# A state-space and token-mixing block: the second quarter of the input by GpSimd, the third quarter and one block of modulation weights at other places

## Chip, cores, metric

The kernel runs on one core of one Trainium2 chip. The metric is device microseconds from the launch to the end. Five engines work side by side: TensorE (PE: matmuls, with its weight loads as PEld), VectorE (DVE), ScalarE (ACT), GpSimd (POOL) and SyncE (SP), which here only issues DMAs. GpSimd issues a few DMAs too. All DMAs run on the core's 16 DMA engines, and so do the packets that bring each engine its instructions.

## What is computed

The reference, cut to what matters here (L = 2048 tokens, D = 448 channels, N = 256 states, F = 1792):

```python
mod = (silu(c) @ w_mod).reshape(1, 6, 1, 448)           # sa, ca, ga, sb, cb, gb
h = layernorm(x) * (1 + ca) + sa
K = 2 * real(einsum("dn,dnl->dl", C, exp(A * dt * pos)))   # one kernel of length L per channel
y = irfft(rfft(h) * rfft(K)) + h * D_skip                # per channel, over the tokens
x = x + ga * y
h = layernorm(x) * (1 + cb) + sb
x = x + gb * (w2.T @ gelu(w1.T @ h + b1) + b2)           # over the tokens
```

## The kernel before

The first half makes the 448 convolution kernels K. Channels are taken 16 at a time in 28 groups, each in two halves of the states: 56 steps, in sets of 8 (`BATCH`). A set begins with a *window* (`window`, slots e = 0 to 7): TensorE makes exponents (`st_exponents`, L621), ScalarE takes Exp of them into `mag` (L644), GpSimd makes `m2` from `mag` (`st_mag2`, L660 and L665), and VectorE does statistics and parameter work between. Then come the set's eight *steps* (`st_step`). In each, ScalarE turns two PSUM tiles of phases, `xe` and `xg`, into sines and cosines (L677 to L682). GpSimd makes the tile `G` (L684, L685), and VectorE makes the tile `E` (L686, L687, then whatever `between` holds, then L689, L690). TensorE makes the next step's phases (`st_phase`, L621) and, two steps later in the first set, 64 small products of E and G (`st_kgen`, L711).

The order on TensorE, VectorE, ScalarE and GpSimd is the order in which the code is written. In this part SP's is too. An engine that waits holds up everything behind it, and a DMA of SP or GpSimd is issued only when its turn comes in that engine's row.

The input x (2048 x 448) is loaded into one tile `xt`, as 16 rows of 128 x 448, in four quarters of four rows: `x_load(r0, n, eng)` issues four DMAs (one for each 32 partitions) of n rows each. Before the change the quarters go out like this. Rows 0 to 3: by GpSimd in `first_chain`. Rows 4 and 5, then 6 and 7: by SP in two calls, ahead of the first window. Rows 8 to 11 and 12 to 15: by GpSimd, behind steps 1 and 2 of the first set (steps count from 0). The layer norm's statistics of a row (`u_stats`, L513 and L514 on VectorE) are placed by hand: rows 0 to 3 in slots 4 to 7 of the first window, rows 2s and 2s + 1 inside step s for s = 2 to 7, by `between`, in the middle of VectorE's work on that step.

The modulation weights come in six blocks of 448 x 448 (`wm_load`). Block 1 is loaded by SP ahead of the first window; block 2 from the table `late`, which runs an entry at the head of step s, here s = 4; block 0 at s = 7. `modulation(k, half)` uses block 1 at steps 4 and 5, block 2 at steps 6 and 7 (L502 and L498 on TensorE). The tables `lph` and `lex`, which TensorE reads for phases and exponents, come by small SP DMAs in between (L607, L611), some of which wait until TensorE has left the buffer.

The second half of the program (inverse transform, second layer norm, the two matmuls with w1 and w2) is untouched by the change.

Of the kernel before, what the change touches and what calls it, by code (L numbers as in the profile page):

```python
# [220 lines left out]
def tile_adaln_s4d_mixer(ctx, tc, i, out):  # L221
# [20 lines left out]
    with ExitStack() as es:  # L242
        V, S, G, T = nc.vector, nc.scalar, nc.gpsimd, nc.tensor
# [53 lines left out]
        def x_load(r0, n, eng=nc.sync):  # L297
            for g in range(4):
                to = xt[32 * g : 32 * g + 32, r0 : r0 + n, 0:D]
                eng.dma_start(to, x.rearrange("(n g r) d -> g n r d", g=4, r=16)[g, :, r0 : r0 + n])  # L300
# [22 lines left out]
        def wm_load(k, tile):  # L323
            wms[k] = tile
            nc.sync.dma_start(wms[k], i["w_mod"][:, k * D : (k + 1) * D].rearrange("(q p) d -> p q d", p=PP))
# [11 lines left out]
        def wm_slot(k):  # L337
            w = wm0.rearrange("p k d -> p (k d)")[0:PP]
            return w[:, 4 * D * (k % 4) : 4 * D * (k % 4 + 1)].rearrange("p (q d) -> p q d", q=4)
# [1 line left out]


        late = {
            4: lambda: wm_load(2, wm_slot(2)),
            7: lambda: wm_load(0, wm_slot(0)),
            6: lambda: [
                nc.sync.dma_start(wu, i["WU"]),
# [114 lines left out]
        def logs(root=False):  # L462

            for a, s, u, xa, ya in tmp.values():
                S.activation(u, ya, AF.Square)
                S.activation(s, s, AF.Ln)
                S.activation(u, u, AF.Ln, bias=1.0)
            if root:
                S.activation(rs, mv[:, :, 1], AF.Ln, bias=eps_t)
                S.activation(rs, rs, AF.Exp, scale=-0.5)  # L470
            for q, (a, s, u, xa, ya) in tmp.items():
                S.activation(a, a, AF.Exp, bias=ldt[:, q : q + 1])
            tmp.clear()

        def angle():

            for a, s, u, xa, ya in tmp.values():
                S.activation(xa, ya, AF.Arctan)
# [134 lines left out]
        def load(g, exps):  # L613
            load_up(g, exps)
            load_lo(g, exps)
# [323 lines left out]
        par_load(1, par_names[2:4])  # L939
        for g in (1, 2):  # L940
            load(g, False)
        x_load(4, 2)
        x_load(6, 2)
        wm_load(1, wm_slot(1))
        remainder()

# [13 lines left out]
        def more(n):  # L960

            for _ in range(n):
                if next(rest, None) in ("logs", "end"):
                    return
# [26 lines left out]
        def window(s):  # L991
            if s:
                aside.append(True)
            angle()
            logs(s == 8)
            if s == 8:
                u_scale()
                u_table(0)
                u_table(1)

            if s == 0:
                st_exponents(s)
            for e in range(BATCH):
                st_exp(s + e)

                if e + 1 < BATCH:
                    st_exponents(s + e + 1)
                else:
                    st_phase(s)
                mellow()  # L1010
                flush(dve)
                flush(act)
                if s == 8 and e == 0:
                    tt(mod[1], mod[1], mod[2], ALU.mult)
                if s < 32:
                    more(WPACE[s // 8][e])
                if s == 0 and e >= 4:
                    u_stats(e - 4)
                if s == 8 and e in (3, 4):
                    modulation(0, e - 3)  # L1020
                if s == 8 and e == 5:

                    G.tensor_tensor(mod[0], mod[0], mod[2], ALU.mult)
                if s and e < (2 if s <= 32 else 1):
                    st_kgen(s - (2 if s <= 32 else 1) + e)
                elif e == 5:
                    if s == 8:
                        yks[0] = y0.tile([P, 32, DC], F32, tag="yk", name="yk0")
                    st_s1(s > 16)

                for k, e0 in ((4, 1), (5, 3), (3, 6)) if s == 16 else ():
                    if e in (e0, e0 + 1):
                        modulation(k, e - e0)

                if s == 8:
                    warm(7)
                if s in (8, 16):
                    some(u_rows, rows, (2, 2, 2, 2, 2, 0, 1, 1)[e])
                elif s == 24 and e != 5:
                    some(u_cols, cols, 1)  # L1040

                if s >= 40 and e == 2:
                    piece(False, True)
                if s >= 40 and e == 4:
                    piece(pieces[0] < NP, True)
                if s == 0 and e > 1:
                    st_mag2(e - 2)
                elif s and (e < 2 or s >= 32):
                    st_mag2(s + e)
                if s == 0 and e == 3:  # L1050
                    for r in range(4):
                        dsk_copy(r)
            aside.clear()
            if s == 0:

                S.activation(one, one, AF.Sin)
# [6 lines left out]
        for s in range(tail):  # L1063
            if s == 32:
                early.close()
                fp = es.enter_context(tc.tile_pool(name="fp", bufs=2))
                m2p.append(right("m2l", BATCH - 3))
                yks[1] = fp.tile([P, 32, DC], F32, name="yk1", bufs=1)
                for n in range(3):
                    pc_load(n)  # L1070
            if s % 2 == 0 and 0 < s and s // 2 + 2 < NG:
                load(s // 2 + 2, False)
            if s == 8:
                first.close()
            if s in late:
                late[s]()
            if s < NHALF and s % BATCH == 0:
                window(s)
                if s == 0:
                    gp_ = right("gp", 3)  # L1080
            if s % BATCH == 4:
                for g in range(s // 2 + 2, min(s // 2 + 6, NG)):
                    load(g, True)

            def between():
                flush(dve)
                if 2 <= s < BATCH:
                    for r in range(2 * s, 2 * s + 2):
                        u_stats(r)
                if s < len(pace):  # L1090
                    more(pace[s])

            mellow()
            if s >= NHALF:
                flush(dve)
                mellow()
            else:
                if s < 32 and s % BATCH > 1:
                    st_kgen(s - 2)
                if s % BATCH < 2:  # L1100
                    warm(10)
                if (s + 1) % BATCH:
                    st_phase(s + 1)
                elif s + 1 < NHALF:
                    st_exponents(s + 1)
                if s == 7:
                    warm(10)

                if s > 32 and s % BATCH:
                    st_kgen(s - 1)  # L1110
                st_step(s, between)
            flush(act)
            if s == NHALF:
                st_kgen(s - 1)


            if s in (1, 2):
                x_load(4 + 4 * s, 4, G)
            free = s > 7 and not st_s1(s % BATCH == BATCH - 1)
            if s + 2 < 32 and (s + 2) % BATCH > 1 and s + 2 > 5:  # L1120
                st_mag2(s + 2)

            if 3 < s < 8:
                modulation(s // 2 - 1, s % 2)
            if s == 7:
                par_load(2)

            if 8 <= s < 16 and free:
                some(u_rows, rows, 2 if s % 2 else 3)
            if s == 12:  # L1130
                par_load(3)
            if s == 16:
                spec.close()
                up = early.enter_context(tc.tile_pool(name="up", bufs=2))
                for n in range(4):
                    u_load(n)
            if 17 <= s < 32 and free:
                some(u_cols, cols, 2 if s < 24 else 3)
            if s == 31:
                flush(dve)  # L1140
                flush(act)
            if s > 32:
                piece(pieces[0] < NP and (s % 2 == 1 or s >= NHALF))
            if s == 34:

                for t in (ft, b1, b2):
                    V.memset(t, 0.0)
                nc.sync.dma_start(ft, i["FT"])
                nc.sync.dma_start(b1, i["B_b1"].rearrange("(t p) -> p t", p=P))
                nc.sync.dma_start(b2, i["B_b2"].rearrange("(t p) -> p t", p=P))  # L1150
# [52 lines left out]
    with ExitStack() as es:  # L1203
        es.enter_context(tc.manual_schedule(engines={ENG.PE, ENG.Activation, ENG.DVE, ENG.Pool}))
        V, S, G = nc.vector, nc.scalar, nc.gpsimd
# [192 lines left out]
```

## Time and profile before

| what | value |
|---|---|
| time, median of 3 runs | 698.07 us (697.39 to 699.43) |
| the profiled execution | 699.5 us, its span 697.7 us |
| busy: PE, PEld | 646.5 us (93%), 486.1 us (70%) |
| busy: DVE, ACT, POOL | 424.1 us (61%), 448.5 us (64%), 274.7 us (39%) |
| moved by DMA | 128.04 MB, mean 184 GB/s |
| granted TensorE clock, mean | 0.988 |

Rows in order of time give the start, the length, the engine, the line and operation, the tile written and those read, shapes, and in brackets how long the engine was idle before and what released it. A group's row gives totals instead. `L300` is line 300 of the kernel before. "issue" as a releaser means that the engine waited for nothing that the profile names. The rows of a table by stretches give, for each engine, busy time and instructions, then TensorE's granted clock, the busy share of the DMA engines and GB/s.

### The profile page before, as it was taken

How to read it: one execution, taken by the hardware profiler on the slowest of the kernel's cores; microseconds unless marked ns; L12 is line 12 of the kernel's file. 1: busy time of each engine (PE TensorE's matmuls, PEld its weight loads, DVE VectorE, ACT ScalarE, POOL GpSimd, SP SyncE). 2: the span in 40 equal slices, each digit the busy share in tenths (PEclk: the TensorE clock that was granted, in tenths of full speed). 3: DMA queues.
4: the chain of work that ended last, by engine and by line, in shares of the span. 5: the costliest groups of instructions: out<-in, count | busy, mean ns of one | idle time of the engine just before them, and what ended most of it. 6: DMA issues, size and time to landing. Idle time of an engine off the chain costs nothing.

```text
span 697.7 us, 18532 instructions
## 1 busy us (share of the span) xinstructions
PE 646.5 (93%) x7314; PEld 486.1 (70%) x7314; DVE 424.1 (61%) x811; ACT 448.5 (64%) x841; POOL 274.7 (39%) x364
## 2 busy tenths in 40 slices
PE   0868999999988899999999989999999999999997
PEld 0444454455545676676789747778999999999996
DVE  7877889787575584857744368777622354444431
ACT  5787698899879899999766568877422332222220
POOL 6694669588588767777546200000000000000000
PEclk9998999999999999999999999999999999999999
DMA  7595647588785486554579899974683445555640
GB/s 183 178 194 143 214 163 241 212 234 268 213 266 165 126 170 170 145 157 120 142 235 301 257 278 244 236 177 135 174 247 108 146 132 159 159 158 165 169 129 28
DMA packets 101894, 128.04 MB, mean 184 GB/s; under 512 B 13547, under 2 KB 85231, under 8 KB 101807
## 3 DMA queue, kind: packets, MB, share of 16 engines
q1 hardware_dynamic: 100606, 123.31, 63.0%
q0 software_dynamic: 1200, 3.54, 2.4%
q8 instruction: 58, 0.95, 0.6%
q14 instruction: 30, 0.24, 0.1%
HBM read 91.46 MB, written 34.87 MB: 181 GB/s over the span
## 4 chain that ended last, share of the span: by engine, by line
PE 68%; ACT 10%; DMA 8%; DVE 6%; issue 4%; POOL 3%; SPq 1%; DVEq 0%; ACTq 0%; POOLq 0%
PE xe L621 7%; PE acc L1222 7%; PE o L1365 6%; PE o L1364 6%; PE o L1366 6%; PE acc L1223 6%; PE acc L1224 6%; PE kg L711 6%; DMA si<-in_SK_dram 3%; PE xg L621 3%; PE pu L542 2%; PE pu L574 2%; PE vv L820 2%; PE kx L804 2%; PE vv L821 2%
## 5 line engine op out<-in xcount | busy, mean ns | idle before, releaser
L206 ACT CAST whi<-w 128x896 fp32r<-128x896 f32 x64 | 59.8, 938 | 134.9 <-PE o L1365 84.6
L215 DVE TENSOR_TENSOR wlo<-w,whi 128x896 fp32r<-128x896 f32 x64 | 68.1, 1088 | 43.1 <-ACT whi L206 36.8
L684 POOL TENSOR_TENSOR G<-mag,gs 128x512 f32<-128x512 f32 x56 | 71.9, 1283 | 50.9 <-ACT gs L680 47.1
L1222 PE MATMUL acc<-h3h,whi 128*128 128x448 f32 x224 | 82.7, 369 | 0.8 <-ACT h3h L1273 0.8
L1223 PE MATMUL acc<-h3l,whi 128*128 128x448 f32 x224 | 81.5, 364 | 0.7 <-DVE h3l L1280 0.5
L1365 PE MATMUL o<-ul,whi 128*128 128x448 f32 x224 | 81.3, 363 | 0.0
L1364 PE MATMUL o<-uh,whi 128*128 128x448 f32 x224 | 81.2, 362 | 0.0
L1224 PE MATMUL acc<-h3h,wlo 128*128 128x448 f32 x224 | 80.7, 360 | 0.0
L1366 PE MATMUL o<-uh,wlo 128*128 128x448 f32 x224 | 80.6, 360 | 0.0
L711 PEld LDWEIGHTS kg<-E,G 128*32 128x32 f32 x3584 | 56.6, 114 | 32.3 <-issue 22.2
L711 PE MATMUL kg<-E,G 128*32 128x64 f32 x3584 | 66.4, 228 | 6.7 <-issue 6.1
L685 POOL TENSOR_TENSOR G<-mag,gs 128x512 f32<-128x512 f32 x56 | 71.8, 1282 | 0.0
L621 PE MATMUL xg<-tab,lph 64*128 64x512 f32 x112 | 62.3, 556 | 5.1 <-ACT gs L680 2.4
L621 PE MATMUL xe<-tab,lph 64*128 64x512 f32 x112 | 62.2, 555 | 1.1 <-ACT gs L681 0.9
L686 DVE TENSOR_TENSOR E<-m,xe 128x512 f32<-128x512 f32 x53 | 36.4, 687 | 41.3 <-ACT xe L679 24.3
L1368 DVE SCALAR_TENSOR_TENSOR y<-o,b,mod 128x448 f32<-128x448 f32 x16 | 10.9, 684 | 80.2 <-PE o L1366 80.2
L665 POOL TENSOR_TENSOR m<-mag,w 128x512 f32<-128x512 f32 x53 | 56.0, 1056 | 4.3 <-DMA u<-us_d 0.2
L1222 PEld LDWEIGHTS acc<-h3h,whi 128*128 128x128 f32 x224 | 42.0, 188 | 13.9 <-ACT h L1278 5.6
L812 DVE TENSOR_TENSOR z<-kx,u 128x448 f32<-128x448 f32 x48 | 28.4, 620 | 27.7 <-PE kx L804 27.7
L1223 PEld LDWEIGHTS acc<-h3l,whi 128*128 128x128 f32 x224 | 42.1, 188 | 3.3 <-DVE h3l L1280 0.8
L1364 PEld LDWEIGHTS o<-uh,whi 128*128 128x128 f32 x224 | 42.0, 188 | 3.4
L621 PE MATMUL xe<-tab,lex 64*128 64x512 f32 x56 | 28.9, 531 | 16.6 <-DMA lex<-wm 15.8
(233 smaller groups left out, 1512.1 us busy)
## 6 DMA issues: line engine op xcount, KB each, us to landing
w<-in_B_w_dram SPq DMA_DIRECT2D x64, 224.0 KB
w<-in_B_w_dram SPq DMA_DIRECT2D x32, 448.0 KB
u<-us_d SPq DMA_DIRECT2D x48, 224.0 KB
yu_d<-yt SPq DMA_DIRECT2D x16, 448.0 KB
yi<-yu_d SPq DMA_DIRECT2D x32, 224.0 KB
us_d<-uo SPq DMA_DIRECT2D x16, 448.0 KB
v_d<-vt SPq DMA_DIRECT2D x32, 224.0 KB
vt<-v_d SPq DMA_DIRECT2D x16, 448.0 KB
```

The lines of the kernel that those rows point to most:

```text
L206: self.nc.scalar.copy(hi, w)
L215: eng.tensor_tensor(lo, w, hi.bitcast(F32), ALU.subtract)
L621: T.matmul(out[k], lhs[r], rhs[r], start=start, stop=stop)
L684: G.tensor_tensor(Gt[:, 1], mg_, v32(sg), ALU.mult)
L685: G.tensor_tensor(Gt[:, 0], mg_, v32(cg_), ALU.mult)
L711: T.matmul(kg[32 * q : 32 * q + 32, m], Gt[:, c, d], E[:, c, d], start=h == 0 and c == 0 and m == 0, stop=h == 1 and c == 1, skip_group_ch ...
L1222: nc.tensor.matmul(acc[f], hi[:, fs], h3h[:, r], start=r == 0, stop=False)
L1223: nc.tensor.matmul(acc[f], hi[:, fs], h3l[:, r], start=False, stop=False)
L1224: nc.tensor.matmul(acc[f], lo[:, fs], h3h[:, r], start=False, stop=r == 15)
L1364: nc.tensor.matmul(o, hi[:, ks], uh[kh][:, k], start=kh == 0 and k == 0, stop=False)
L1365: nc.tensor.matmul(o, hi[:, ks], ul[kh][:, k], start=False, stop=False)
L1366: nc.tensor.matmul(o, lo[:, ks], uh[kh][:, k], start=False, stop=kh == 1 and k == 6)
```

## The change

Three places of the code change, and a fourth is only written anew. SP no longer loads rows 4 to 7: GpSimd does, in slot 6 of the first window, four rows a DMA. Rows 8 to 11 are loaded behind step 0 instead of step 1. Rows 12 to 15 stay behind step 2 (8 + 2 x 2 = 12). Block 2 of the modulation weights is loaded at the head of step 3 instead of step 4.

```diff
         late = {
-            4: lambda: wm_load(2, wm_slot(2)),
+            3: lambda: wm_load(2, wm_slot(2)),
...
             load(g, False)
-        x_load(4, 2)
-        x_load(6, 2)
         wm_load(1, wm_slot(1))
...
                     more(WPACE[s // 8][e])
+                if s == 0 and e == 6:
+                    x_load(4, 4, G)
                 if s == 0 and e >= 4:
                     u_stats(e - 4)
...
-            if s in (1, 2):
-                x_load(4 + 4 * s, 4, G)
+            if s in (0, 2):
+                x_load(8 + 2 * s, 4, G)
```

In GpSimd's row, the end of the first window: each pair of L660 and L665 makes one step's `m2` (steps 3 and 4 here; steps 3 to 5 keep it in a part of the tile `wm`).

```order
 L660 TENSOR_TENSOR w<-mag 128x16
 L665 TENSOR_TENSOR wm_79<-mag,w 128x512
+L300 DMA xt<-in_A_u_dram 32x4x448 x4
 L660 TENSOR_TENSOR w<-mag 128x16
 L665 TENSOR_TENSOR wm_79<-mag,w 128x512
```

Four DMA issues now stand ahead of the pairs of steps 4 and 5.

GpSimd's row in the first steps, from step 0's G on (a pair of L684 and L685 is one step's G):

```order
 L684 TENSOR_TENSOR G<-mag,gs 128x512
 L685 TENSOR_TENSOR G<-mag,gs 128x512
-L684 TENSOR_TENSOR G<-mag,gs 128x512
-L685 TENSOR_TENSOR G<-mag,gs 128x512
 L300 DMA xt<-in_A_u_dram 32x4x448 x4
 L684 TENSOR_TENSOR G<-mag,gs 128x512
 L685 TENSOR_TENSOR G<-mag,gs 128x512
+L684 TENSOR_TENSOR G<-mag,gs 128x512
+L685 TENSOR_TENSOR G<-mag,gs 128x512
 L300 DMA xt<-in_A_u_dram 32x4x448 x4
 L684 TENSOR_TENSOR G<-mag,gs 128x512
```

The third quarter's four issues moved from behind step 1's G to behind step 0's; the fourth quarter's stay behind step 2's.

SP's row from the last table load ahead of the first window to the tables of the second set (`wm_79` from `in_w_mod` is a block of modulation weights, `lph` and `lex` are tables):

```order
 L611 DMA lph_144<-pars_57 64x1x256
-L300 DMA xt<-in_A_u_dram 32x2x448 x8
 L325 DMA wm_79<-in_w_mod_dram 112x4x448
 L607 DMA lph_142<-pars_57 32x256
 L611 DMA lph_142<-pars_57 64x1x256
+L325 DMA wm_79<-in_w_mod_dram 112x4x448
 L607 DMA lph_143<-pars_57 32x256
 L611 DMA lph_143<-pars_57 64x1x256
-L325 DMA wm_79<-in_w_mod_dram 112x4x448
 L607 DMA lex_145<-pars_57 32x256
```

The eight input issues are gone, and block 2 stands ahead of one pair of table loads that it stood behind.

## Prediction

> **What bounds the kernel now.** I read the page first (engines, DMA queues, chain), then the waits of the early stretch, then each engine's rows in order of time. The page's rows for the engines, the instruction queue and the chain:
>
> ```profile
> PE 646.5 (93%) x7314; PEld 486.1 (70%) x7314; DVE 424.1 (61%) x811; ACT 448.5 (64%) x841; POOL 274.7 (39%) x364
> ...
> q8 instruction: 58, 0.95, 0.6%
> ...
> PE 68%; ACT 10%; DMA 8%; DVE 6%; issue 4%; POOL 3%; SPq 1%; DVEq 0%; ACTq 0%; POOLq 0%
> ```
>
> PE carries two thirds of the chain, but the change touches only the first 65 us, where the input and the modulation weights come in. So that stretch has to be read by itself. The longest waits between 36 and 63 us (engine, line, what it waited for; total, times, longest):
>
> ```profile
> DVE st L513 <- DMA xt<-in_A_u_dram: 4.6, 1, 4.6
> PE kg L711 <- issue: 4.2, 1, 4.2
> ```
>
> VectorE waits once for input rows. The rows in order of time show where: L686 opens the VectorE part of a step, and L513 is the statistics of one input row.
>
> ```profile
> 37.92 0.69 DVE L686 TENSOR_TENSOR E<-m,xe 128x512 f32<-128x512 f32 x1 [0.41 <-ACT xe L679]
> ...
> 39.12 0.62 DVE L513 BATCH_NORM_STATS2 st<-xt 128x6 f32<-128x448 f32 x1
> ...
> 45.62 0.68 DVE L686 TENSOR_TENSOR E<-wm,xe 128x512 f32<-128x512 f32 x1
> 46.22 0.68 DVE L687 SCALAR_TENSOR_TENSOR E<-mag,xe 128x512 f32<-128x512 f32 x1
> 51.52 0.63 DVE L513 BATCH_NORM_STATS2 st<-xt 128x6 f32<-128x448 f32 x1 [4.62 <-DMA xt<-in_A_u_dram]
> ...
> 54.18 0.68 DVE L686 TENSOR_TENSOR E<-wm,xe 128x512 f32<-128x512 f32 x1
> ...
> 62.94 0.69 DVE L686 TENSOR_TENSOR E<-m,xe 128x512 f32<-128x512 f32 x1 [0.99 <-issue]
> ```
>
> The reader is to see the beat: steps 2 and 3 together take 45.62 - 37.92 = 7.70 us, 3.85 each, and VectorE never pauses in them. Step 4 takes 8.56, because at 46.90 the third quarter of the input (rows 8 to 11) is not there. The second quarter was needed at 39.12 and was there. VectorE sets the pace here, so these 4.62 us are on the path, unless something else is late at the same moment. Something is: the chain of waits shows TensorE stopped for nearly the same time.
>
> ```profile
> 48.06 0.88 PE kg L711 x58
> 48.93 4.23 issue
> 53.16 0.43 PE kg L711 x6
> ```
>
> It stops after 58 of 64 products of one step and waits for nothing that the profile names. The page has 58 instruction packets of 0.95 MB together, 16.4 KB each; 14,628 matmuls and weight loads over 58 are 252 instructions a packet. The DMA rows (packets, MB, share) of the stretches 37 to 40 and 40 to 50 us, and the instruction row of 50 to 52; queue 0 is GpSimd's, queue 1 SP's, queue 8 TensorE's instructions:
>
> ```profile
> q1 hardware_dynamic: 430, 0.74, 88.2%
> q8 instruction: 1, 0.02, 1.9%
> ```
> ```profile
> q0 software_dynamic: 281, 1.06, 56.5%
> q1 hardware_dynamic: 658, 0.97, 50.1%
> q14 instruction: 1, 0.01, 0.4%
> ```
> ```profile
> q8 instruction: 1, 0.02, 4.1%
> ```
>
> No instruction packet moves from 40 to 50, and the next comes just before TensorE resumes. In the stretches 37 to 44 and 44 to 49 it ran (matmuls, then loads):
>
> ```profile
> 37.00:44.00 7.00, 5.29 (x142) 3.50 (x135) 6.49 (x14) 6.78 (x15) 6.99 (x11) 0.92 1.01 236
> 44.00:49.00 5.00, 4.93 (x118) 3.09 (x110) 2.87 (x6) 3.73 (x9) 4.99 (x5) 0.77 1.08 204
> ```
>
> That is 505 instructions, two packets' worth, with one packet in. So I read the 4.23 us as instructions queued behind the same loads. Both stalls have one cause: too many bytes asked for at once.
>
> **The change part by part.** GpSimd's rows in time order, from the end of the first set to the fourth quarter's issue:
>
> ```profile
> 26.80 0.42 POOL L660 TENSOR_TENSOR w<-mag 128x16 f32<-128x16 f32 x1
> ...
> 28.63 1.05 POOL L665 TENSOR_TENSOR wm<-mag,w 128x512 f32<-128x512 f32 x1
> 31.09 1.27 POOL L684 TENSOR_TENSOR G<-mag,gs 128x512 f32<-128x512 f32 x1 [1.42 <-ACT gs L680]
> 32.32 1.32 POOL L685 TENSOR_TENSOR G<-mag,gs 128x512 f32<-128x512 f32 x1
> 35.13 1.29 POOL L684 TENSOR_TENSOR G<-mag,gs 128x512 f32<-128x512 f32 x1 [1.48 <-ACT gs L680]
> 36.37 1.29 POOL L685 TENSOR_TENSOR G<-mag,gs 128x512 f32<-128x512 f32 x1
> 37.60 2.20 POOL L300 DMA_DIRECT2D xt<-in_A_u_dram  x4
> 39.81 1.29 POOL L684 TENSOR_TENSOR G<-mag,gs 128x512 f32<-128x512 f32 x1
> ...
> 42.26 2.20 POOL L300 DMA_DIRECT2D xt<-in_A_u_dram  x4
> ```
>
> *GpSimd's queue.* Four issues cost 2.20 us of it. The second quarter now goes out at 26.8; the two m2 pairs behind it end at 29.68 + 2.20 = 31.9, and step 0's G starts 0.8 late and ends near 34.4. The third quarter follows, 34.4 to 36.6 (before, 37.6 to 39.8). Step 1's G ends near 39.1 (before, 37.66), step 2's starts there (before, 39.81), and the fourth quarter goes out at 41.6 (before, 42.26). So TensorE gets step 1's G about 1.4 us later, behind VectorE's beat, which turns to the next step only near 41.8 (37.92 + 3.85) anyway; from step 2 GpSimd is 0.7 us ahead. I cost this at nothing; without that cover it is 1.4 us.
>
> *SP's queue,* from the same view:
>
> ```profile
> 29.45 0.54 SPq L611 DMA_DIRECT2D lph<-pars  x1
> 30.03 6.09 SPq L300 DMA_DIRECT2D xt<-in_A_u_dram  x8
> 36.16 0.43 SPq L325 DMA_DIRECT2D wm<-in_w_mod_dram  x1
> ...
> 39.55 0.46 SPq L325 DMA_DIRECT2D wm<-in_w_mod_dram  x1
> ```
>
> Eight issues of 6.09 us go. The first weights (modulation 1) leave at 30.0, not 36.2. Modulation 2's leave after the two lph loads of step 2, which wait for TensorE to leave that buffer (about 33), so near 34, not 39.55: now ahead of the third quarter.
>
> *The bytes.* Slices of 5 us; the last three columns are TensorE's granted clock, the DMA engines' busy share and GB/s:
>
> ```profile
> 30.00:35.00 5.00, 4.49 (x24) 2.19 (x22) 4.36 (x6) 4.06 (x10) 2.55 (x2) 1.00 0.67 176
> 35.00:40.00 5.00, 4.78 (x144) 3.36 (x144) 4.55 (x10) 4.78 (x11) 4.86 (x7) 1.00 0.62 172
> 40.00:45.00 5.00, 3.29 (x72) 2.28 (x71) 4.90 (x11) 4.37 (x9) 4.99 (x7) 0.79 1.08 218
> 45.00:50.00 5.00, 3.93 (x81) 2.21 (x75) 1.90 (x4) 4.17 (x9) 4.92 (x6) 0.87 1.06 190
> ```
>
> The engines are two thirds busy from 30 to 40 and full from 40 to 50, at 204 GB/s on average. The change adds no byte; it fills the slack. In the new order, from about 29 us: a quarter of the input (128 x 4 x 448 x 4 B = 0.92 MB), two weight blocks (112 x 4 x 448 x 4 B = 0.80 MB each), the third quarter (0.92 MB): 3.44 MB, with some 0.15 MB of lph loads. At 204 GB/s that is 17.6 us, so the third quarter lands near 46.6, against 46.9 when VectorE asks. Bounds from the nearest rows: at 218 it is 45.5, at 190 it is 47.9. So the wait of 4.62 becomes 0 to 1.0; I take 0.3, and the term is **-4.3 us**. The second quarter goes out 26.8 to 29.0 with at most the first weights beside it, 1.72 MB, which 204 GB/s moves by 37.4; it is needed at 39.12. I cost that at nothing; at 172 GB/s it is 39.0, still in time.
>
> *TensorE's instructions.* This is the term that comes back. The packet that came at 37 to 40 was asked for when the engines had about one weight block ahead; now it meets what is left of 3.44 MB. By 36.7 some 7.7 us x 204 = 1.57 MB are through, so 1.9 MB stand ahead of it. Before, the second packet was asked for, by my reading, one packet's worth of instructions (252) ahead of the stop at 48.9, near 43.5 (44 to 49 holds 228). It met modulation 2's weights and the third and fourth quarters, 2.64 MB, less 3.5 us x 218 = 0.76 that were through: 1.9 MB too. It moved after 50, some 6.5 us later. If the first is as late, it moves near 43.2, and TensorE, which resumed up to 3.2 us after the slice's start at 50, has it by 43 to 46.4, where 43.4 is when it needs it: 0 to 3.0 us lost, of which about 1 is cover (the next tiles are ready for VectorE that long before its turn). The second packet, asked for at 43.5 to 45, meets about 1.4 MB (rest of the third quarter, the fourth, table loads): 1.4/1.9 x 6.5 = 4.8 us, so TensorE goes on near 51.5, where VectorE's beat without a stall has room until about 49.5 (45.62 + 3.85). The two overlap, so the later one counts: 0 to 4 us, and I take **+1.9**, half of the stop that the trace shows.
>
> *Half clock.* The granted clock was 0.79 and 0.87 in those slices and 1.00 around them. A shorter stop may spare some of it; step 7's 0.99 us wait (L686 at 62.94) came behind that. Bounds 0 to -1.0; I take **-0.2**.
>
> *Weights of modulation 2* are used by TensorE only at step 6, behind step 4's stall; moving the load costs nothing by itself beyond the bytes above.
>
> **Sum:** -4.3 + 1.9 - 0.2 = -2.6 us. The profiled execution took 699.5 us (span 697.7), so 696.9; the median of the three runs is 1.4 below it, 698.07, so 695.5. The rest of the chain follows in order behind this stretch, so I let the gain pass to the end.
>
> **The rivals.**
>
> *A, instructions never wait.* The trace shows 10 us without an instruction packet under full DMA engines. [...] As a mechanism of this kernel: if the stop at 48.9 was an accident of one engine's backlog, only VectorE's wait counted and all of it goes: 4.62 plus up to 1.0, 692.5 to 693.5. For it: a packet did come within 37 to 40 at 88% busy.
>
> *B, the stall moves.* The third quarter lands no earlier in effect, or both instruction packets are as late as before: TensorE then resumes near 53 as now, and 4.3 comes back whole: 697 to 699. For it: the bytes are the same, and modulation 2's weights are now ahead of the third quarter.
>
> *C, slower.* The place is TensorE's first packet, in step 3. If it waits as the longest shown (10 us from the 37 to 40 slice, so until 47 to 48), TensorE stops for 4 to 5 us at 43.4, the second packet is asked for only then and meets the fourth quarter: another 5 us, until 56 to 57 instead of 53.16: 3 to 4 us slower, 701 to 702. It decides from a delay of 8.5 us for the first packet. Against it: the same amount of bytes delayed the other by 6.5.
>
> *D, the change does nothing:* the second quarter is late at 39.12 by what the third gains. The bytes above speak against it; it would give 698, with B.
>
> **How the numbers follow.** Forecast 0.45 at 695.5 (its own range 694 to 696.8); A 0.18; B with D 0.29; C 0.08. A measurement of this kernel tells about 0.3% (2.1 us) from no change. Faster: A and three quarters of the forecast's case and some of B, 0.55; slower: C and a tail of B, 0.09; the rest 0.36. The range for 8 in 10 goes from A's middle to B's end: 692.8 to 699.0.
>
> **What would show it.** Right: no wait of L513 for xt over 1 us; GpSimd's second-quarter issue between two m2 pairs near 27; the engines busy over 0.9 from 30 to 48; L686 of step 5 at 50 to 52 (before, 54.18); a shorter "issue" wait of kg L711 in one or two places between 43 and 52. Wrong: L513 still waiting over 2 us at step 2 or 4; an "issue" wait over 4 us near 43; or L686 of step 7 earlier by 3 us or more and the end not, which would mean that the gain is lost behind this stretch.

## The result, and the profile after

The changed kernel takes 699.81 us (median of 12 runs, 694.38 to 702.48), the kernel before 698.77 (12 runs, 697.15 to 702.83). The means are 699.34 and 699.36; the ratio is 1.0001, its 95% interval 0.9979 to 1.0023. No gain of over 1.5 us and no loss of over 1.6 us is left by that interval. The forecast was 2.6 us faster. The runs of one kernel lie up to 8 us apart and follow TensorE's mean granted clock: in the changed kernel's 12 runs from 694.38 us at 0.993 to 702.48 at 0.985 (correlation -0.90), in the 35 runs of the kernel before that stand beside the first experiments -0.88.

The profiled execution took 699.92 us, its span 698.1, mean granted clock 0.985 (before 0.988). On the page of after, the engines' totals and the chain are those of before:

```profile
PE 645.8 (93%) x7314; PEld 484.9 (69%) x7314; DVE 424.2 (61%) x811; ACT 448.2 (64%) x841; POOL 276.9 (40%) x368
...
PE 71%; ACT 11%; DMA 6%; DVE 5%; issue 4%; POOL 2%; SPq 1%; DVEq 0%; ACTq 0%; POOLq 0%
```

What moved shows only in the early stretch. VectorE's rows of after, in order of time (L686 opens a step, L513 reads an input row):

```profile
31.64 0.69 DVE L686 TENSOR_TENSOR E<-m,xe 128x512 f32<-128x512 f32 x1 [2.86 <-ACT xe L679]
...
40.09 0.69 DVE L686 TENSOR_TENSOR E<-m,xe 128x512 f32<-128x512 f32 x1 [1.10 <-ACT xe L679]
...
47.83 0.68 DVE L686 TENSOR_TENSOR E<-wm,xe 128x512 f32<-128x512 f32 x1
...
49.03 0.62 DVE L513 BATCH_NORM_STATS2 st<-xt 128x6 f32<-128x448 f32 x1
...
52.34 0.69 DVE L686 TENSOR_TENSOR E<-wm,xe 128x512 f32<-128x512 f32 x1 [0.58 <-issue]
...
60.04 0.68 DVE L686 TENSOR_TENSOR E<-m,xe 128x512 f32<-128x512 f32 x1
```

L513 no longer waits for input at step 4. The opening rows are those of steps 0, 2, 4, 5 and 7. Step 2 begins 2.17 us later than before (40.09 against 37.92), step 7 2.90 earlier (60.04 against 62.94). Step 0 already begins 1.04 later (31.64 against 30.60), and GpSimd came to the place of the moved issue 0.89 later (27.69 against 26.80), so about half of the 2.17 is older than the change's first effect. Between step 2 and step 7 the wait of 4.62 went. Something new came ahead of step 2: the waits of TensorE from 36 to 63 us name it.

```profile
PE xg L621 <- DMA lph<-pars: 2.7, 1, 2.7
PE kg L711 <- issue: 1.6, 1, 1.6
```

Before, only "issue" stood there with 4.2. The chain of after shows where that table was:

```profile
29.21 8.04 DMA lph<-pars
37.39 0.39 PE xg L621
```

The table of step 2 (64 KB) was asked for at 29.21 and took 8.04 us. GpSimd's row of after tells what went out just ahead of it:

```profile
27.69 2.20 POOL L300 DMA_DIRECT2D xt<-in_A_u_dram  x4
```

That is the second quarter of the input, 0.92 MB. The wait of 2.69 is not the table's price, though. The tiles `xg` have two buffers (the pool `pph`), so step 2's phases also need VectorE's last product of step 0 (L690) to be done. Where nothing else is late, TensorE's product starts 0.10 us behind it, as in the kernel before:

```profile
34.44 0.68 DVE L690 TENSOR_TENSOR E<-m,xg 128x512 f32<-128x512 f32 x1
```
```profile
35.22 0.47 PE L621 MATMUL xg<-tab,lph 64*128 64x512 f32 x1 [0.73 <-ACT gs L680]
```

After:

```profile
35.93 0.68 DVE L690 TENSOR_TENSOR E<-m,xg 128x512 f32<-128x512 f32 x1
```
```profile
37.39 0.47 PE L621 MATMUL xg<-tab,lph 64*128 64x512 f32 x1 [2.69 <-DMA lph<-pars]
```

There TensorE could have started near 36.7, so the table cost 0.7 us of its own. The stretches of after, to be read beside the same ones of before (clock, DMA share and GB/s last):

```profile
30.00:35.00 5.00, 4.70 (x29) 2.64 (x27) 3.33 (x4) 4.88 (x11) 4.84 (x6) 1.00 0.98 221
35.00:40.00 5.00, 2.61 (x71) 2.04 (x71) 3.99 (x7) 2.86 (x7) 4.80 (x7) 0.88 1.08 238
40.00:45.00 5.00, 4.56 (x88) 2.48 (x80) 4.84 (x10) 4.19 (x9) 4.42 (x6) 0.78 1.07 219
45.00:50.00 5.00, 2.86 (x74) 1.77 (x72) 4.90 (x12) 3.69 (x8) 4.99 (x5) 0.90 0.99 202
```

The slack from 30 to 40 (0.67 and 0.62 before) is filled, as forecast. Part of the 2.90 goes with TensorE's clock: from the opening of step 5 to that of step 7 before took 8.76 us and after 7.70, and there before ran at half clock and after did not. The stretch 53 to 60 us, first of before, then of after:

```profile
53.00:60.00 7.00, 6.79 (x80) 3.62 (x79) 6.90 (x16) 3.93 (x8) 3.19 (x5) 0.51 0.35 84
```
```profile
53.00:60.00 7.00, 6.71 (x175) 3.82 (x164) 6.86 (x16) 7.00 (x16) 6.28 (x7) 1.00 0.21 63
```

In this pair of profiles the 2.90 us then go at two places, both with TensorE at half clock. The stretches 69 to 73 and 144 to 148 us, first of after, then of before:

```profile
69.00:73.00 4.00, 4.00 (x81) 2.87 (x81) 3.00 (x6) 1.62 (x4) 3.55 (x6) 0.57 0.49 175
144.00:148.00 4.00, 4.00 (x28) 1.55 (x29) 3.37 (x6) 3.97 (x9) 3.92 (x5) 0.57 0.88 209
```
```profile
69.00:73.00 4.00, 2.49 (x71) 1.25 (x72) 2.44 (x8) 3.96 (x10) 2.53 (x5) 1.00 0.14 44
144.00:148.00 4.00, 3.31 (x47) 1.73 (x50) 3.03 (x5) 3.97 (x9) 3.92 (x5) 1.00 1.07 244
```

A clock of 0.57 over 4.00 us is 4.00 x 0.43 x 2 = 3.44 us at half rate; the clock records of the trace have 0.50 for 3.41 us from 69.48 and from 144.58. Matched instruction by instruction on VectorE, after is 2.8 us ahead when the second window begins (before's 66 to 71 us), 1.3 ahead from 88 to 151, 0.2 behind from 166 to 195, and 0.4 behind at the end. What sets such a stretch off is not shown: between 62.5 us and the one at 69.48 TensorE's longest pause is 1.63 us.

Whether these stretches are the cause of the loss, or one throw of a die, two profiles can't tell. The means of the clock speak against them as the usual cause: 0.9865 in the 12 runs of after, 0.9877 in the 35 runs of before. By the line through those 35 runs (517 us for each unit of clock) the difference is worth an estimated 0.6 us, not 2.9. The rest was tried.

### The profile page after: what moved, and what is told of

Its sections match the earlier page's. It is cut to its first block, busy times and chain, and to the rows that moved or that the text cites. A ratio compares the mean times of both kernels' runs of the same rounds, so it can differ in the third digit from the quotient of the medians.

```text
span 698.1 us, 18532 instructions
## 1 busy us (share of the span) xinstructions
PE 645.8 (93%) x7314; PEld 484.9 (69%) x7314; DVE 424.2 (61%) x811; ACT 448.2 (64%) x841; POOL 276.9 (40%) x368
## 4 chain that ended last, share of the span: by engine, by line
PE 71%; ACT 11%; DMA 6%; DVE 5%; issue 4%; POOL 2%; SPq 1%; DVEq 0%; ACTq 0%; POOLq 0%
PE xe L621 7%; PE o L1365 6%; PE acc L1222 6%; PE o L1364 6%; PE o L1366 6%; PE acc L1223 6%; PE acc L1224 6%; PE kg L711 6%; PE vv L820 3%; PE kx L804 3%; PE vv L821 3%; PE pu L542 2%; PE pu L574 2%; PE xg L621 1%; PE kg L633 1%
## 5 line engine op out<-in xcount | busy, mean ns | idle before, releaser
L684 POOL TENSOR_TENSOR G<-mag,gs 128x512 f32<-128x512 f32 x56 | 72.0, 1286 | 44.3 <-ACT gs L680 44.3
L685 POOL TENSOR_TENSOR G<-mag,gs 128x512 f32<-128x512 f32 x56 | 71.9, 1283 | 0.0
L686 DVE TENSOR_TENSOR E<-m,xe 128x512 f32<-128x512 f32 x53 | 36.3, 685 | 40.8 <-ACT xe L679 23.6
L665 POOL TENSOR_TENSOR m<-mag,w 128x512 f32<-128x512 f32 x53 | 55.8, 1053 | 4.2 <-POOL w L660 0.2
```

Of the source, the lines that this page charges most:

```text
L684: G.tensor_tensor(Gt[:, 1], mg_, v32(sg), ALU.mult)
L685: G.tensor_tensor(Gt[:, 0], mg_, v32(cg_), ALU.mult)
```

## The experiments

Two sets of theories were put on record: C (the early gain is taken back by half-clock stretches behind later pauses of TensorE) against N (the waits only change places); then, with sharper numbers, L (gained early, lost behind) against M (the bytes of the rush from 30 to 50 us set the stretch whatever their order, so little is gained, and what is gained there passes to the end). Each group of kernels was run beside the kernel before, whose median in that group is its base.

### Each part alone

`x_only` is the changed kernel without the move of the weights, `wm_only` the kernel before with that move alone:

```diff
-            3: lambda: wm_load(2, wm_slot(2)),
+            4: lambda: wm_load(2, wm_slot(2)),
```

> The changed kernel with block 2 of the modulation weights back at step 4. Theory C (the change gains about 3 us in the first 68 us and half-clock slices behind later pauses of TensorE take it back): this keeps the gain or adds to it, since the third quarter and the instruction packets have 0.8 MB less ahead of them; step 7 of the first set ends by 64 us (before 66.9, changed 64.0), the issue wait of kg L711 near 46 us falls from 1.6 to under 1 us, the time is 696 to 699 us with the scatter of the changed kernel. Theory N (the change gains nothing, the waits only move): VectorE waits again for input rows or TensorE for instructions, 698 to 700 us, and step 7 ends at 66 us or later.

> The kernel before with only block 2 of the modulation weights one step earlier (step 3). Both theories: no gain; 0.8 MB more stand ahead of the third quarter's last parts, so VectorE's wait for input rows at step 4 is 4 to 6 us (before 4.6) and the time is 698 to 700 us. A time under 697 us would mean that the weights' place, not the input's, carries the change.

Measured: 699.47 us (ratio 1.0001, 0.9976 to 1.0027) and 697.92 (1.0003, 0.9972 to 1.0033), before 698.52 in 35 runs. Neither part does anything alone that can be told. The longest waits named for DMAs and for nothing ("issue") from 33 to 63 us, first of `x_only`, then of `wm_only`:

```profile
PE kg L711 <- issue: 4.5, 1, 4.5
PE xg L621 <- DMA lph<-pars: 3.8, 1, 3.8
```
```profile
PE kg L711 <- issue: 5.0, 1, 5.0
DVE st L513 <- DMA xt<-in_A_u_dram: 2.0, 1, 2.0
```

With GpSimd's early quarter comes the wait for the table, without it the one for the input. TensorE's stop for nothing named stays in both. In `x_only` VectorE ends step 7 at 67.06 and the stop is 4.5: these are N's signs (66 or later; C had 64 and under 1). In `wm_only` the input wait of 2.0 missed the expected 4 to 6, and 697.92 lies just under the expected 698 to 700.

### TensorE kept busy

Eleven and eight more filler matmuls in the second window and in step 17, where the half-clock stretches of after lay, in the changed kernel (`warm_after`) and in the one before (`warm_before`):

```diff
                 if s == 8:
-                    warm(7)
+                    warm(7 if e else 18)
...
-                    warm(10)
+                    warm(18 if s == 17 else 10)
```

> The changed kernel with filler matmuls (results never read) in two pauses of TensorE: 11 more in the second window's first slot, 8 more in step 17, about 1.4 and 1.0 us. Theory C: the half-clock slices at 69 and 145 us no longer come, the mean granted clock rises from 0.985 to 0.989 or more, and the median falls by 2 to 4 us to 695 to 698 us. Theory N: the fillers change nothing or cost their own time, 699 to 702 us.

> The kernel before with the same fillers. Theory C: its profiled execution had no half-clock slice at those two pauses, so it gains less than the changed kernel does, 0 to 2 us: 697 to 699 us, and the changed kernel with fillers is 2 to 3 us faster than this one. Theory N: the two kernels with fillers are equal within 1 us.

Measured: 702.63 us (1.0043, 1.0015 to 1.0071) and 702.65 (1.0043, 1.0017 to 1.0068). The remedy failed and costs both the same, some 3 us by the ratios and 4 by the medians. One place of the cost is a wait that neither kernel had, from 76 to 92 us (here of `warm_after`):

```profile
DVE yt L545 <- DMA yu_d<-yt: 4.0, 1, 4.0
PE y L749 <- DVE yt L545: 3.6, 1, 3.6
```

Half-clock stretches still came in these runs (mean clock 0.981 and 0.985 in the profiles; 0.87 from 78 to 88 us in `warm_after`). C's forecast missed (no rise of the clock, no gain), and N's came true but for the time, 0.6 above its range. Still C is not refuted: the fillers brought a cost of their own.

### The first stretch by itself, first try

The kernels were stopped after step 7 (what is left out is in the expectations):

```diff
+            if s == 7:
+                break
```

> The kernel before, stopped after step 7 of its main loop: steps 8 and later, the spectral part behind them and the dense layers are left out, and 128 rows of the input are stored in place of the result. It times the first stretch by itself, with little of the scatter of 8 us that the whole kernel shows from run to run. VectorE's last product of step 7 ended at 66.87 us in the profile of before, so some 70 to 73 us in all. Theory L (the change gains early and loses it behind this stretch) and theory M (the early waits only change places, and the 2.8 us between the two profiles are chance) both expect this; it is the base for the three beside it.

> The changed kernel, stopped after step 7 in the same way. Theory L: 2.0 to 3.0 us below the shortened kernel before, as the two profiles show at step 7. Theory M: within 0.7 us of it, since TensorE's wait of 2.7 us for the phase table of step 2 takes the place of VectorE's wait for the input.

> The changed kernel with modulation 2's weights back at step 4, stopped after step 7. Theory L: most of the gain is the input's, so 1.5 to 3 us below the shortened kernel before. Theory M: within 0.7 us of the shortened kernel before. If the weights' place carries the gain: within 0.5 us of the shortened kernel before while the whole change is 2 us or more below it.

> The changed kernel with the second quarter issued by GpSimd behind the last m2 pair of the first set and not ahead of its last two pairs, so near 29.7 us, after the loads of step 2's phase table were asked for at 29.2; stopped after step 7. If TensorE's wait of 2.7 us for that table holds the start of every later step: 1.5 to 2.7 us below the shortened changed kernel. If the next wait in line (TensorE's instructions, or VectorE for the second quarter) stands just behind it: within 0.7 us of the shortened changed kernel.

Measured: 72.89 us (71.23 to 73.94), 71.71 (71.41 to 72.19), 72.18 (71.76 to 72.82), 72.62 (72.27 to 73.20). The changed one is 1.2 below by medians, but that is no gain: four of the six runs of `cut_before`, the profiled one (73.94) among them, lie 1.7% or more above its fastest, and its other two, 71.23 and 71.35, lie below all five of the changed kernel. `cut_q2_late` missed both of its forecasts, 0.9 above `cut_after`. Its table was asked for at 25.66, 1.5 us ahead of the quarter, and landed at 29.92 by its completion signals (semaphore events kept in the trace), after 4.3 us and not 8.04. TensorE stood at the same xg product all the same,

```profile
34.71 0.48 PE L621 MATMUL xg<-tab,lph 64*128 64x512 f32 x1 [3.71 <-issue]
```

for nothing that the profile names, but again 0.10 us behind the end of VectorE's last product of step 0:

```profile
33.94 0.67 DVE L690 TENSOR_TENSOR E<-m,xg 128x512 f32<-128x512 f32 x1
```

So there VectorE was the next wait in line. It was late because one of its operations, L413, took 2.69 us (0.71 before, 1.15 in after); why stays open. These kernels ended with loads, some 7 us behind VectorE's last product, so they were made again without those.

### The first stretch without late loads, and with fewer bytes

`end7_before` and `end7_after` drop the loads of step 7 as well; `less7_before` and `less7_after` also the weights of modulations 1 and 2:

```diff
-            7: lambda: wm_load(0, wm_slot(0)),
...
-        wm_load(1, wm_slot(1))
+        wms[1] = wms[2] = xt[0:112, 0:4, 0:D]
```

> The kernel before, stopped after step 7 of its main loop, and without the loads that the earlier shortened kernels still had under way at their end (modulation 0's weights, the third parameter block; the store is one row): so it ends with VectorE's and GpSimd's work of step 7. Left out are also steps 8 and later, the spectral part and the dense layers. Both theories below: 65 to 69 us, from VectorE's end of step 7 at 64.5 us in the first shortened kernel; it is the base for the three beside it.

> The changed kernel stopped and cleared of late loads in the same way. Theory L (the change gains early and loses it behind this stretch): 2.0 to 3.0 us below the base. Theory M (the early waits only change places, because the same bytes stand ahead of the phase table and of TensorE's instructions): between 1.0 below and 0.7 above it. The earlier shortened pair lay 0.9 us apart in its means, with loads at the end that blur it.

> The base with modulations 1 and 2 multiplying by rows of the input that are there already, so that their weights (two blocks of 0.80 MB) are not loaded. Theory M, in which the bytes of this stretch set its length whatever their order: 2 us or more below the base, since 1.6 MB at 204 GB/s are 7.9 us of full engines, and the stops of VectorE for the input and of TensorE for its instructions fall below 1 us. If the waits come from the order of the issues and not from the bytes: within 1 us of the base.

> The changed kernel stopped after step 7, without the weights of modulations 1 and 2 in the same way. Theory M: within 0.7 us of the base without these weights, as with few bytes the place of the second quarter does not matter, and 1.5 us or more below the shortened changed kernel. If the order of the issues is what counts: as far below the base without weights as the changed one lies below the base, 2 us by theory L.

Measured: 66.97 us (66.32 to 67.15) and 66.42 (65.77 to 66.69); without the weights 61.87 (61.71 to 61.97) and 61.43 (61.13 to 61.73). So 1.6 MB less give 5.1 and 5.0 us, and the change gives 0.55 and 0.44. The waits from 26 to 66 us, first of `end7_before`, then of `end7_after`, then of `less7_before` (line numbers shifted by one to two):

```profile
DVE st L512 <- DMA xt<-in_A_u_dram: 3.7, 1, 3.7
PE kg L710 <- issue: 3.7, 1, 3.7
```
```profile
PE xg L620 <- DMA lph<-pars: 2.5, 1, 2.5
PE kg L710 <- issue: 1.7, 2, 1.2
```
```profile
DVE st L511 <- DMA xt<-in_A_u_dram: 0.3, 1, 0.3
```

In the kernel before, the input wait and TensorE's stop hang on the bytes (3.7 and 3.7 against 0.3 and none); in `less7_after` a stop of 1.5 stays. The stretch 45 to 50 us of `end7_before`, then of `less7_before`, shows it too: engines full at 1.06 in the one, 0.22 busy in the other, where VectorE never pauses (4.90 of 5.00). The table's wait hangs on them less surely: neither profile without weights names it, but in `less7_after` the load of step 2's table still took 7.0 us by its completion signals (25.70 to 32.70).

```profile
45.00:50.00 5.00, 1.35 (x66) 0.94 (x59) 1.66 (x5) 3.39 (x7) 4.92 (x6) 1.00 1.06 227
```
```profile
45.00:50.00 5.00, 4.18 (x96) 2.36 (x92) 4.90 (x11) 4.58 (x11) 4.92 (x6) 1.00 0.22 55
```

The 0.55 has to be read with care. In `end7_after` VectorE was done at 61.19 and a last load was not:

```profile
60.51 0.68 DVE L689 TENSOR_TENSOR E<-m,xg 128x512 f32<-128x512 f32 x1
```
```profile
62.00:63.00 1.00, 0.00 (x0) 0.00 (x0) 0.00 (x0) 0.00 (x0) 0.00 (x0) 0.84 0.10 30
```

In `end7_before` VectorE's last product ended at 63.77, so by VectorE's end of step 7 the change gains 2.6 us in this pair of profiles. That is not steady. `warm_before` and `warm_after` have the code of before and after up to step 7, and there step 7 opens 0.46 us later with the change (61.05 against 60.59). From opening to opening of VectorE's steps (L686; L685 in the `end7` kernels), in us:

| steps | 0 to 2 | 2 to 4 | 4 to 5 | 5 to 7 | 0 to 7 |
|---|---|---|---|---|---|
| before | 7.32 | 7.70 | 8.56 | 8.76 | 32.34 |
| after | 8.45 | 7.74 | 4.51 | 7.70 | 28.40 |
| `warm_before` | 7.32 | 7.70 | 6.75 | 8.04 | 29.81 |
| `warm_after` | 10.51 | 8.15 | 3.84 | 7.70 | 30.20 |
| `end7_before` | 6.98 | 7.70 | 7.66 | 8.91 | 31.25 |
| `end7_after` | 7.95 | 7.78 | 4.62 | 8.00 | 28.35 |

In all three pairs the change gains at step 4 (2.9 to 4.0 us) and loses around step 2 (1.0 to 3.2). The whole stretch is shorter by 3.9 and 2.9 us in two pairs and longer by 0.4 in the third. So the early gain on average is some 2 us with a wide scatter, and the timed pairs show 0.4 to 0.6; the runs don't narrow it further.

### The weights later

If the bytes hold the stretch, the weights might come behind it, where the engines are a fifth busy (0.21 from 53 to 60 us in after). `spread_after` and `spread_before` load them between the exponent tables that SP asks for at the end of step 4, and compute both modulations in steps 6 and 7; the two `end7` kernels are the same, shortened.

```diff
                 for g in range(s // 2 + 2, min(s // 2 + 6, NG)):
                     load(g, True)
+                    if g in (4, 6):
+                        wm_load(g // 2 - 1, wm_slot(g // 2 - 1))
...
-            if 3 < s < 8:
-                modulation(s // 2 - 1, s % 2)
+            if 5 < s < 8:
+                modulation(1, s % 2)
+                modulation(2, s % 2)
```

> The changed kernel, whole, with the weights of modulations 1 and 2 loaded between the exponent tables at the end of step 4 (some 45 and 52 us) and both modulations computed in steps 6 and 7. Theory M (the bytes of the rush from 30 to 50 us set the stretch, and a gain there passes to the end): 3 to 5 us below the kernel before, 693.5 to 695.5 where that one takes 698.5. Theory L (what is gained early is lost behind step 8): within 1.5 us of the kernel before.

> The kernel before, whole, with the weights and the two modulations moved in the same way, and the input as before. Theory M: 3 to 5 us below the kernel before, and within 1 us of the changed kernel with the same move, since the place of the second quarter counts for 0.5 us. Theory L: within 1.5 us of the kernel before.

> The changed kernel with the weights moved in that way, stopped after step 7 without the late loads: steps 8 and later, the spectral part and the dense layers are left out. Theory M: near the shortened changed kernel without these weights, 61.4 to 63.5 us, against 66.4 with the weights in the rush. If loading them later only stops TensorE or VectorE later, in steps 5 to 7: 65 us or more.

> The kernel before with the weights moved in that way, stopped after step 7 without the late loads; the same parts are left out. Theory M: 61.9 to 64 us, against 67.0 with the weights in the rush. If loading them later only stops an engine later: 65.5 us or more.

Measured: 707.50 us (1.0125, 1.0085 to 1.0166), 708.49 (1.0127, 1.0088 to 1.0166), 69.77 (67.81 to 70.81) and 71.55 (70.27 to 72.98); in both shortened kernels most runs lie over 1.2% above the fastest, but the fastest too are slower than the kernels with the weights in the rush (66.42 and 66.97). Both theories missed by their sign; only the fallback of the shortened pair, a stop at a later place, came true. TensorE's rows of `spread_after` give the reason:

```profile
53.50 0.58 PE L620 MATMUL xg<-tab,lph 64*128 64x512 f32 x1 [4.81 <-issue]
58.00 0.96 PE L501 MATMUL pm<-wm,scb 112*32 112x448 f32 x8
62.13 0.96 PE L501 MATMUL pm<-wm,scb 112*32 112x448 f32 x8 [3.17 <-DMA wm<-in_w_mod_dram]
```

The first stop, for nothing named, is longer than before's 4.23: SP asks for both blocks in the rush still (42.18 and 46.19). The second block is late: TensorE stands for it in step 6, and the second window stands behind TensorE. VectorE's row there in `spread_after`:

```profile
71.98 0.17 DVE L517 TENSOR_TENSOR nm<-rs 128x16 f32<-128x16 f32 x1 [7.47 <-ACT rs L469]
```

Before, this wait was 2.63. Matched on VectorE, `spread_after` is 5.9 us behind before from 76 us of before's time on and 7.6 at the end: a loss made here does reach the end.

### Does a gain made here reach the end?

`less_before` is the whole kernel before without the loads of these weights (the edit of `less7_before`, no stop). `early1_after` is the changed kernel with block 1 asked for by GpSimd near 18 us:

```diff
                 if s == 0 and e > 1:
                     st_mag2(e - 2)
+                    if e == 2:
+                        wm_load(1, wm_slot(1), G)
```

> The kernel before, whole, but modulations 1 and 2 multiply by rows of the input that are there already, so their weights (1.6 MB) are not loaded; everything else is computed. The shortened pair differed by 5.0 us. Theory M (a gain of the stretch passes to the end): 4 to 6.5 us below the kernel before. Theory L (it is lost behind step 8): within 2 us of it.

> The changed kernel, whole, with the weights of modulation 1 issued by GpSimd near 18 us, behind the first m2 pair of the first set, where the DMA engines are a third busy, and not by SP near 30. Half of the 1.6 MB leaves the rush. Theory M: half of the 5 us, so 1.5 to 3 us below the kernel before, unless the block delays the parameter tables that the first set stores and loads between 18 and 25 us, by up to its own 4 us: then 0 to 2 us above it. Theory L: within 1.5 us of the kernel before.

Measured: 695.48 us (692.32 to 698.47; ratio 0.9964, 0.9943 to 0.9985) and 696.93 (693.11 to 701.62; 0.9982, 0.9953 to 1.0011), before 697.98 in 23 runs. The first saves 2.5 us, 1.0 to 4.0 by the interval: its middle lies between L (within 2) and M (4 to 6.5), and its ends touch both; the 5 us of the shortened pair are outside. Its profile shows the gain passing whole: VectorE's last product of step 7, first of before, then of `less_before`,

```profile
66.19 0.68 DVE L690 TENSOR_TENSOR E<-m,xg 128x512 f32<-128x512 f32 x1
```
```profile
61.09 0.68 DVE L689 TENSOR_TENSOR E<-m,xg 128x512 f32<-128x512 f32 x1
```

5.10 us apart, and the spans 697.7 and 692.5, 5.2 apart, at a mean clock of 0.995. Behind step 7 before has two half-clock stretches of 3.41 us by its clock records, at 220.36 and 237.43; the mean of 0.995 over the 692.5 us of `less_before` comes to some 6.9 us at half rate, as much. So in this pair nothing in the order of the work takes the gain back. But the pair is a lucky one: the profiled run of before is 1.5 us above its median, that of `less_before` 1.2 below its own, and by the medians half of the gain is missing. `early1_after` is 1.05 us below before and within its scatter. The table's wait is still there from 26 to 66 us,

```profile
PE xg L621 <- DMA lph<-pars: 1.9, 1, 1.9
```

and no version that surely beats both kernels came out of this.

## Why the prediction was wrong

**VectorE's input wait: right.** It was put at 4.62 to 0.3 and is 0; the third quarter was there at 49.03.

**Weights and bytes: right.** The engines are full from 30 us on (0.98 to 1.08 busy up to 50), and modulation 2's weights went out at 34.06.

**TensorE's instructions: near in size, the cause not shown.** +1.9 was taken for two late packets, the first 0 to 3.0 us late from 43.4, the second until 51.5. After shows one stop of 1.56, at 46.23 by the chain, and none near 51. VectorE's only wait near it is the 0.58 at the opening of step 5. That the stop is a wait for instructions was the author's reading: after's queue 8 has one packet at 44 to 45 us and the next at 49 to 50, and TensorE goes on at 47.80, between them; in before the packets are at 38 to 39 and 50 to 51, and it goes on at 53.16.

**Half clock: too small.** -0.2 was taken, within 0 to -1.0. From step 5 to step 7 after is 1.06 us quicker (granted clock 1.00 from 53 to 60 us, before 0.51), `warm_after` 0.3, and `end7_after` 0.9 (1.00 from 50 to 60 us, `end7_before` 0.53 and 0.79).

**The second quarter costed at nothing: the failed term.** "The second quarter goes out 26.8 to 29.0 with at most the first weights beside it [...] I cost that at nothing." The quarter itself was in time at 41.29. But from step 0 to step 2 the changed kernels take 1.1, 3.2 and 1.0 us longer than their partners, 1.8 on average. What was not asked is what stands behind the quarter: SP's load of step 2's table, 64 KB, which took 8.04 us. TensorE's wait for it is named with 2.7 us in after, 3.8 in `x_only`, 4.2 in `warm_after`, 2.5 in `end7_after`. Its price beyond VectorE's own lateness is 0.7 us in after, 2.1 in `warm_after` (VectorE's product of step 0 ends at 35.75, TensorE's starts at 37.94) and 0.8 in `end7_after` (33.22, 34.16). The cause of the rest of the 1.8 stays open. The working followed GpSimd's row behind the moved issues and SP's large loads, but not SP's small loads at 29 us.

**The sum at step 7: right by luck.** -2.6 was forecast, and after's step 7 opens 2.90 earlier. But that is -4.05 at step 4 (the input's 4.62 less the 0.58), -1.06 from step 5 to step 7, +1.13 from step 0 to step 2, +0.04 from step 2 to step 4 and +1.04 that step 0 was late already, against -4.3, -0.2, +1.9 and nothing. In the `warm` pair the same code gives +0.46.

**"The rest of the chain follows in order behind this stretch, so I let the gain pass to the end": the second step that failed, in this pair.** The prediction named its sign: step 7 earlier by some 3 us and the end not. In the two profiles the 2.90 went at 69 to 73 and 144 to 148 us, with the clock at 0.57. That half-clock stretches take the gain on average is not shown: the mean clocks leave them some 0.6 us, and the fillers that by theory C should have prevented them cost more than they could save. Shown is that 5.0 us gained early are worth 2.5 (1.0 to 4.0) at the end over 12 runs, and that the change as a whole is worth nothing that 12 runs against 12 can tell (1.5 us). How the missing part divides between a smaller early gain and the clock stays open.

**The rivals.** A (only VectorE's wait counts) fell by TensorE's stop of 1.56. B (the stall moves), at 697 to 699, is nearest to the time and has half the reason: a stall did move, to steps 0 to 2, a place it didn't name. C did not happen: its place, TensorE's stop in step 3, cost 1.56 and not 4 to 5. D's cause, the quarter late at its use, did not happen.

## What to carry over

When a load is moved earlier, list every small load that is asked for just behind it, on other queues too, and who waits for it: here 64 KB behind 0.92 MB took 8.04 us, and the steps that needed it gave back 1.0 to 3.2 us of the 2.9 to 4.0 gained. A wait's length is not its price (2.7 us named, 0.7 paid in after): ask what the engine would have waited for next. In this crowded stretch, where several waits meet, moving bytes inside it shifted the wait, and taking 1.6 MB out shortened it by 5 us; but a place behind it must also be ahead of the use (TensorE stood 3.17 us for the second block in `spread_after`). One pair of profiles is one throw: the same stretch came out 3.9 us shorter, 2.9 shorter and 0.4 longer. And know first what the end can show: with runs of one kernel 8 us apart, a gain under 2 us needs its own short kernel, one whose last instruction is the work in question and not a load.

## What the hardware showed unexpectedly

A 64 KB load, asked for 1.5 us behind the first of four 0.23 MB loads on another queue, took 8.04 us in after; asked for 1.5 us ahead of them it took 4.3 in `cut_q2_late`.

The completion signals in the traces, which no view prints, show more. The second block of weights in `spread_after`, asked for at 46.19, sends 16 signals: 14 between 54.93 and 56.82, the last two at 61.01 and 62.09, and TensorE's wait for it ends at 62.13. The table's load at 29.21 in after sends three, one at 30.22 and two at 36.85 and 37.26. The first block of weights in after, asked for at 30.90, has the same form: 14 signals between 37.41 and 39.38, two more at 45.16 and 46.86. What holds the last signals back is not shown.

TensorE's granted clock falls to 0.50 for stretches of 3.41 or 6.83 us, at other places from profile to profile: by the clock records in before at 42.87, 53.11 (the 6.83), 220.36 and 237.43, in after at 38.76, 49.00, 69.48, 144.58 and 219.67 (the 6.83). TensorE's rows have the same group of four products at both rates, first in after, then in before:

```profile
144.40 3.22 PE L574 MATMUL pu<-yi,s 128*128 128x448 f32 x4
```
```profile
145.84 1.74 PE L574 MATMUL pu<-yi,s 128*128 128x448 f32 x4
```

This shows in the time of the whole: the mean granted clock of a run, 0.980 to 0.995, goes with 8 us of 698.
